# One product's form, a rider limit and a redrawn order of work in a gated mix of two attention blocks

## The chip, the cores and the metric

The kernel runs on one core of a Trainium2 chip. A core has five engines that run side by side, each through its own queue of instructions in order: PE (TensorE, matmuls, with a row PEld for the loading of weights), DVE (VectorE), ACT (ScalarE), POOL (GpSimd) and SP (SyncE, which here issues nearly all DMAs). The metric is the device time of one execution in microseconds. The time before is 739.46 us, the median of three runs (739.46, 739.46 and 740.83).

## What is computed

```python
def reference(A_x, A_wqkv, A_wo, B_x, B_wqkv, B_wo, gate_w):
    x = A_x                                     # [1, 2048, 512]
    g = sigmoid((x * gate_w).sum(-1, keepdims=True))
    a = A(x, A_wqkv, A_wo)     # full attention: 32 heads of 16, softmax over all 2048 keys
    b = B(x, B_wqkv, B_wo)     # 32 heads; each query sees 8 keys, at offsets 0, 2, ..., 14 behind it
    return g * a + (1 - g) * b
```

A and B each project x to q, k and v, attend, and multiply by their `wo`. B_x is not read. Nearly all the work is branch A's: 32 heads x 2048 x 2048 exponentials, and the two matmuls around them.

## The kernel before

**Branch A.** The 2048 queries are cut in 4 chunks of 512, the heads in 8 groups of 4. A *period* is one chunk with one group, 32 periods in all; within a period there are 16 key tiles of 128 by 4 heads, so 64 *units* of 128 keys x 512 queries of one head. For each unit PE writes the scores (tile `ring` or `m_ps`, in PSUM), an engine turns them into exponentials, and PE multiplies those by the values (tile `vp_row`) and adds them up in `acc`. Two engines make exponentials:

- ACT, which reads a whole *set* of ring banks with one instruction (`act_source`, tile `pT`). There are two sets, rA and rB, of three banks of 512 columns; a set holds three units of ACT, or two.
- DVE, in *quads*: the four heads of one key tile (`make_quad`, line 1673). Four conversions (`conv`, line 1707) turn scores into the bits of a power of two with one multiply and add; two further instructions (`term`, line 1723) add offsets to those bits, and PE adds the three terms with weighted copies of the values (`vd_row`). All these write tile `dt`.

The scores of a quad's head are filled either into the single bank `m_ps`, which all projections share too, or as a *rider* into the third bank of a ring set, whose other two banks then hold units of ACT (`rider`, line 1472; `take_ride`, line 1503). A set is filled again only when both ACT's exponential and the rider's conversion have read it.

**Branch B.** For each of 16 tiles of 128 queries (`b_tile`, line 945) PE projects q, k and v, the keys and values go to DRAM, and come back shifted (tiles `ksh`, `vsh`). POOL multiplies and adds up the scores (`prod`, `lg`), DVE takes maxima, ACT the exponentials, POOL weighs the values. In `sm_sum` (line 1093) DVE does three small things in a row: it sums the eight exponentials of each of 32 heads (`ssum`), takes the reciprocal (`rr`), and multiplies it in place by the column `ratio` of this tile (128 x 32 elements). POOL's `sm_norm` waits for that product.

**The order of work.** The kernel is written out by a planner (`Sched`) when the program is built. Every piece of work is an `Op` with an engine, a charged duration, what it depends on, buffers that it takes and gives back, and a due time; the planner simulates the five engines and issues the ops in the order in which it starts them. So each engine's queue has one fixed order, and a chain of no-sync dependencies keeps it. `sm_sum` is charged 900 ns as one op. DVE ops that are marked `lock` are kept clear of POOL's instructions; `sm_sum` is not one of them.

What the planner prefers is a `Policy` (line 125): how many quads may be open, how early or late things are pulled, how much PE is to stream before it adds matmuls on zeros (*zero passes*, `acc<-ones_t,zw`; the threshold is raised by `warm`). Time is cut in stretches of 8 us (`STRETCH`, line 68), and the table `CHOICES` gives a seed for each: a seed draws each setting with a chance of 0.3 from its other values; seed 0 takes the usual ones. `turn` (line 194) changes the policy at each stretch. Two settings matter here:

- `ride` (lines 136 and 156): a unit may ride if its conversion, at 683 ns, would end at most so many ns after the fill is visible (lines 1486 to 1489). Riders start after 17.5 us.
- `late` (lines 135 and 152): in `start_quad` (line 1641), `over` is the time that ACT still needs for the period (two periods, when looking one ahead), and `ends` is the time until DVE would have ended one more quad behind all that is due on it. Line 1661 skips the quad:

```python
            if over + S_.policy.late < ends:
                continue
```

All instructions carry line 511 in the profile, that of the helper which records them; they are told apart by their tiles.

Of the kernel before, what the change touches and what calls it, by code (L numbers as in the profile page):

```python
# [11 lines left out]
ALU = mybir.AluOpType  # L12
# [7 lines left out]
H = 32  # L20
# [16 lines left out]
def _mean_log_ratio():  # L37
    n = 4096
    acc = 0.0
    for k in range(n):  # L40
        y = 128.0 * k / n
        s = 0.0
        for o, w in zip(OFFS, WTS):
# [23 lines left out]

STRETCH = 8000.0
CHOICES = (
# [8 lines left out]
YIELD = 150.0  # L78
PARTS = ("k2", "q2", "v2", "bk2", "bv2", "bq2")
LRED = 4000.0  # L80
# [5 lines left out]
def _ap(base, dims):  # L86
    return bass.AP(tensor=base.tensor, offset=base.offset, ap=[list(d) for d in dims])


class Op:  # L90
# [4 lines left out]
    def __init__(self, eng, fn, dur=0.0, mms=None, deps=(), due=None, allow=1000.0, acq=(), rel=(), lat=0.0,  # L95
                 name="", not_before=0.0, after=None, begun=(), prompt=False,
                 lock=False):
        self.eng, self.fn, self.dur, self.mms = eng, fn, dur, mms
        self.deps = [d for d in deps if d is not None]
        self.due, self.allow, self.acq, self.rel, self.lat = due, allow, list(acq), list(rel), lat  # L100
        self.begun = [d for d in begun if d is not None]
        self.start = self.fin = self.vis = None
        self.prompt = prompt
        self.zeros = 0
        self.choose = None
        self.closing = False
        self.lock = lock
        self.gap = 30.0
        self.name, self.not_before, self.after = name, not_before, after
# [19 lines left out]
class Policy:  # L129
    __slots__ = ("full", "press", "quads", "backlog", "heed", "near", "shift", "conv", "ring", "rng", "wobble", "warm", "tight", "late", "whole", "split", "ride")  # L130

    def __init__(self, seed):
        self.full, self.press, self.quads, self.backlog, self.heed = 5, -2000.0, 3, 3000.0, True
        self.near, self.shift, self.conv, self.ring, self.wobble, self.warm = 60.0, 0.0, -5000.0, 480.0, 0.0, 0.0
        self.tight, self.late, self.whole, self.split = 600.0, 2000.0, False, False
        self.ride = 900.0
        self.rng = random.Random(seed)
        if seed:
            def pick(usual, *others):
                return self.rng.choice(others) if self.rng.random() < 0.3 else usual  # L140
            self.full = pick(5, 4)
            self.press = pick(-2000.0, -30000.0)
            self.quads = pick(3, 2, 4)
            self.backlog = pick(3000.0, 1500.0, 4500.0, 6000.0)
            self.heed = pick(True, False)
            self.near = pick(60.0, 20.0, 150.0)
            self.shift = pick(0.0, -4000.0, -2000.0, 2000.0, 4000.0)
            self.conv = pick(-5000.0, 0.0)
            self.ring = pick(480.0, 560.0, 650.0)
            self.wobble = pick(0.0, 500.0, 2000.0)  # L150
            self.tight = pick(600.0, 150.0, 1500.0)
            self.late = pick(2000.0, 0.0, 4000.0)
            self.whole = pick(False, True)
            self.split = pick(False, True)
            self.warm = pick(0.0, 0.04, 0.08, -0.03)
            self.ride = pick(900.0, 700.0, 1100.0)

    def move(self):
        return self.shift + self.wobble * (2.0 * self.rng.random() - 1.0)
# [288 lines left out]
def kernel(  # L448
# [66 lines left out]
    V = Chained(nc.vector, "dve")  # L515
# [72 lines left out]
    ratio = const.tile([128, NT], FP32, name="ratio")  # L588
# [356 lines left out]
    def b_tile(t, due):  # L945
# [147 lines left out]
        def sm_sum():  # L1093
            ssum = work.tile([128, H], FP32, name="ssum", tag="ssum", bufs=2)
            V.tensor_reduce(out=ssum[:], in_=st["lg"][:], axis=AX.X, op=ALU.add)
            rr = work.tile([128, H], FP32, name="rr", tag="rr", bufs=2)
            V.reciprocal(out=rr[:], in_=ssum[:])
            V.tensor_scalar(out=rr[:], in0=rr[:], scalar1=ratio[:, t:t + 1], scalar2=None, op0=ALU.mult)
            st["rr"] = rr

        def sm_norm():
# [2 lines left out]
        s_ = padd(sm_sub, 628.0, after_last=False, early=True, deps=[m_])  # L1104
        x_ = S_.add(Op("ACT", sm_exp, dur=391.0, allow=500.0, deps=[s_], name="smexp"))
        d_ = S_.add(Op("DVE", sm_sum, dur=900.0, allow=2500.0, deps=[x_] + g_done, name="smsum"))
        padd(sm_norm, 628.0, deps=[d_])

# [766 lines left out]
```

## Time and profile before

| | before |
|---|---|
| median of 3 runs | 739.46 us |
| the profiled execution | 737.08 us |
| its span, first to last instruction | 735.3 us |
| mean granted PE clock | 0.997 |
| busy share PE / DVE / ACT / POOL | 91% / 94% / 97% / 56% |
| exponentials on ACT | 648 instructions, 705.2 us |
| conversions on DVE, from ring and m_ps | 403 and 105 |

A line of a group reads: line, engine, operation, tile written <- tiles read, shapes and type, count | busy us in all, mean ns of one | idle time of the engine just before them and what ended it. Rows of a timeline give start and length in us, engine, operation, tiles, shapes and count, and in brackets how long the engine had been idle before, and who ended that. Rows of waits give who waited for whom: us in total, times, the longest.

### The profile page before, as it was taken

How to read it: one execution, taken by the hardware profiler on the slowest of the kernel's cores; microseconds unless marked ns; L12 is line 12 of the kernel's file. 1: busy time of each engine (PE TensorE's matmuls, PEld its weight loads, DVE VectorE, ACT ScalarE, POOL GpSimd, SP SyncE). 2: the span in 40 equal slices, each digit the busy share in tenths (PEclk: the TensorE clock that was granted, in tenths of full speed). 3: DMA queues.
4: the chain of work that ended last, by engine and by line, in shares of the span. 5: the costliest groups of instructions: out<-in, count | busy, mean ns of one | idle time of the engine just before them, and what ended most of it. 6: DMA issues, size and time to landing. Idle time of an engine off the chain costs nothing.

```text
span 735.3 us, 19566 instructions
## 1 busy us (share of the span) xinstructions
PE 672.6 (91%) x8164; PEld 247.3 (34%) x8164; DVE 690.4 (94%) x1234; ACT 713.8 (97%) x675; POOL 415.1 (56%) x418
## 2 busy tenths in 40 slices
PE   8999899989998989999989899899998999989997
PEld 4333232333323223333424233323333333323334
DVE  5999999999999999999799999999999999998994
ACT  4999999999999999999999999999999999999996
POOL 2036465565764656656656557566756676355560
PEclk9999999999999999999999999999999999999999
DMA  9242010030241303040112312120403030300300
GB/s 244 92 68 89 16 40 21 16 115 2 74 87 58 81 2 116 16 121 18 61 57 74 101 59 73 59 66 22 123 23 116 23 123 31 116 1 17 122 9 30
DMA packets 72312, 47.43 MB, mean 64 GB/s; under 512 B 33056, under 2 KB 69408, under 8 KB 72224
## 3 DMA queue, kind: packets, MB, share of 16 engines
q1 hardware_dynamic: 70496, 45.66, 21.0%
q8 instruction: 64, 1.05, 0.6%
q10 hardware_dynamic: 1728, 0.52, 0.3%
q14 instruction: 24, 0.20, 0.1%
HBM read 38.80 MB, written 6.32 MB: 61 GB/s over the span
## 4 chain that ended last, share of the span: by engine, by line
ACT 51%; DVE 25%; PE 11%; issue 10%; SPq 1%; DMA 0%; DVEq 0%; POOL 0%; ACTq 0%
ACT pT L511 51%; DVE dt L511 15%; PE ring L511 4%; PE m_ps L511 4%; PE acc L511 3%; DVE rr L511 2%; DVE kt_all L511 1%; DVE qt L511 1%; DVE lg L511 1%; SPq L511 1%; DVE kvs L511 1%; DVE accT L511 1%; DVE kmax_all L511 1%; DVE vp_row L511 1%; DMA xT<-in_A_x_dram 0%
## 5 line engine op out<-in xcount | busy, mean ns | idle before, releaser
L511 ACT ACTIVATE pT<-ring 128x1024 bf16<-128x1024 f32 (+1 forms) x648 | 705.2, 1285 | 6.5 <-PE ring L511 5.4
L511 PE MATMUL ring<-qt,kt_all 32*128 32x512 bf16 x1943 | 264.9, 383 | 42.0 <-ACT pT L511 30.1
L511 DVE TENSOR_SCALAR dt<-ring 128x512 uint16<-128x512 f32 x403 | 269.8, 677 | 15.1 <-PE ring L511 12.6
L511 POOL TENSOR_TENSOR prod<-ksh,qb 128x512 f32<-128x512 bf16 x128 | 145.5, 1156 | 114.9 <-DVE dt L511 94.2
L511 PEld LDWEIGHTS <-kt_all 32*128 32x128 bf16 (+1 forms) x2304 | 91.8, 91 | 276.2 <-issue 171.2
L511 DVE TENSOR_SCALAR dt<-dt 128x2048 uint16<-128x2048 uint16 x254 | 177.0, 710 | 1.2 <-PE acc L511 0.3
L511 POOL TENSOR_TENSOR vsh<-vsh,lg 128x512 bf16<-128x512 bf16 x128 | 137.4, 1098 | 69.6 <-DVE dt L511 54.3
L511 PE MATMUL acc<-pT,vp_row 128*32 128x512 bf16 x1540 | 156.5, 387 | 2.4 <-ACT pT L511 1.3
L511 POOL TENSOR_TENSOR prod<-prod 128x512 f32<-128x512 f32 x76 | 83.8, 1108 | 66.0 <-DVE dt L511 55.3
L511 PEld LDWEIGHTS <-vp_row 128*32 128x32 bf16 x2048 | 50.7, 94 | 98.6 <-issue 87.8
L511 PE MATMUL acc<-dt,vd_row 128*32 128x512 bf16 x1016 | 82.2, 380 | 0.0
L511 DVE TENSOR_SCALAR dt<-m_ps 128x512 uint16<-128x512 f32 x105 | 71.0, 676 | 0.5 <-PE ring L511 0.4
L511 PE MATMUL m_ps<-bw,xT 128*32 128x512 bf16 x768 | 55.4, 382 | 2.7 <-DVE dt L511 1.9
L511 PE MATMUL acc<-dt,vp_row 128*32 128x512 bf16 x508 | 50.4, 385 | 0.9 <-DVE accT L511 0.9
L511 PE MATMUL m_ps<-qt,kt_all 32*128 32x512 bf16 x105 | 39.9, 380 | 5.5 <-DVE dt L511 3.1
L511 PEld LDWEIGHTS <-xT 128*32 128x32 bf16 (+1 forms) x1088 | 32.9, 96 | 33.3 <-issue 26.6
L511 PE MATMUL m_ps<-ident,vsh 128*128 128x128 bf16 x512 | 37.9, 220 | 1.1 <-DVE dt L511 1.0
L511 DVE TENSOR_REDUCE lg<-prod 128x32 f32<-128x512 f32 x52 | 34.1, 671 | 0.0
L511 PEld LDWEIGHTS <-vsh 128*128 128x128 bf16 x512 | 29.1, 98 | 13.7 <-issue 12.6
L511 PEld LDWEIGHTS <-vd_row 128*32 128x32 bf16 x1016 | 26.1, 97 | 22.1 <-issue 7.7
L511 PE MATMUL acc<-ones_t,zw 128*32 128x512 bf16 x368 | 32.0, 385 | 0.1
L511 POOL TENSOR_TENSOR ott<-accT,rden 128x512 bf16<-128x512 f32 (+1 forms) x16 | 16.9, 1056 | 22.2 <-DVE dt L511 19.2
(94 smaller groups left out, 396.9 us busy)
## 6 DMA issues: line engine op xcount, KB each, us to landing
ksh<-kv_scr SPq DMA_DIRECT2D x16, 1024.0 KB, 5.4
vsh<-kv_scr SPq DMA_DIRECT2D x16, 1024.0 KB, 5.5
kv_scr<-kvs SPq DMA_DIRECT2D x16, 256.0 KB, 2.0
out_dram<-osb SPq DMA_DIRECT2D x14, 128.0 KB, 1.7
bw<-in_B_wqkv_dram SPq DMA_DIRECT2D x1, 1536.0 KB, 8.4
xn<-in_A_x_dram SPq DMA_DIRECT2D x2, 512.0 KB, 4.3
bwo<-in_B_wo_dram SPq DMA_DIRECT2D x1, 512.0 KB, 6.8
woarr<-in_A_wo_dram SPq DMA_DIRECT2D x8, 64.0 KB, 2.4
```

What stands on the lines that cost most here:

```text
L511: return chain_on(key, f(*a, **k))
```

## The change

Three places of the code change.

```diff
 CHOICES = (
-           0, 671811, 186164, 451001, 281332, 80945, 95777, 2725, 841250, 226619, 39723, 166693,
...
-           0, 741684, 0, 650854, 0, 988031, 0)
+           0, 0, 499928, 803669, 208658, 178077, 0, 998560, 158866, 788054, 313197, 966231,
...
+           13420, 0, 869455, 338121, 12097, 448362, 0)
@@ class Policy
-        self.ride = 900.0
+        self.ride = 1050.0
...
-            self.late = pick(2000.0, 0.0, 4000.0)
+            self.late = pick(2000.0, 0.0, 4000.0, -2000.0)
...
-            self.ride = pick(900.0, 700.0, 1100.0)
+            self.ride = pick(1050.0, 850.0, 1250.0)
@@ def sm_sum
-            V.tensor_scalar(out=rr[:], in0=rr[:], scalar1=ratio[:, t:t + 1], scalar2=None, op0=ALU.mult)
+            r1 = ratio[:, t:t + 1]
+            V.tensor_tensor(out=rr[:], in0=rr[:], in1=_ap(r1, [list(r1.ap[0]), [0, H]]), op=ALU.mult)
```

The product in `sm_sum` is written as a product of two tensors, of which the second is the column of the ratio read 32 times, in place of a product with a scalar per partition. The usual value of `ride` goes from 900 to 1050 ns, and its other values from 700 and 1100 to 850 and 1250; `late` may also be drawn as -2000. The table keeps its 91 entries of 8 us; 8 of them were 0, now 9 are. The new seeds draw `ride` 850 ten times, 1050 64 times and 1250 17 times (before: 700 ten, 900 59, 1100 22 times), `late` -2000 nine times, 0 15, 2000 57 and 4000 ten times (before: 0 twelve, 2000 69, 4000 ten times), and a raised `warm` 25 times (before 19). The charge for the clock that the change's name mentions stands in no line of the kernel.

12 rows, old and new, of the table CHOICES are left out of this document.

## The prediction

> **What bounds the kernel now.** I read the page first: the span, the busy shares, the chain that ended last.
>
> ```profile
> span 735.3 us, 19566 instructions
> PE 672.6 (91%) x8164; PEld 247.3 (34%) x8164; DVE 690.4 (94%) x1234; ACT 713.8 (97%) x675; POOL 415.1 (56%) x418
> ...
> ACT 51%; DVE 25%; PE 11%; issue 10%; SPq 1%; DMA 0%; DVEq 0%; POOL 0%; ACTq 0%
> ACT pT L511 51%; DVE dt L511 15%; PE ring L511 4%; PE m_ps L511 4%; PE acc L511 3%; DVE rr L511 2%; DVE kt_all L511 1%; DVE qt L511 1%; DVE lg L511 1%; SPq L511 1%; DVE kvs L511 1%; DVE accT L511 1%; DVE kmax_all L511 1%; DVE vp_row L511 1%; DMA xT<-in_A_x_dram 0%
> ```
>
> Two engines share the exponentials of branch A, and both are nearly full: ACT (tile pT) and DVE (tile dt). Next come two stretches, the middle of the run and 3.2 us out of it, then the mean clock. Columns: length, then for PE, PEld, DVE, ACT and POOL the busy time with its count, then granted clock, DMA share, GB/s.
>
> ```profile
> 25.00:700.00 675.00, 620.08 (x7501) 221.19 (x7500) 650.89 (x1156) 669.50 (x631) 396.35 (x387) 1.00 0.21 62
> ```
> ```profile
> 656.60:659.80 3.20, 3.20 (x30) 0.79 (x26) 2.18 (x5) 1.90 (x3) 1.09 (x1) 0.50 0.00 0
> ```
> ```profile
> core 0: 735.3 us, clock 0.997
> ```
>
> From 25 to 700 us ACT is idle for 675.00 - 669.50 = 5.5 us, DVE for 24.1 us. So the time is ACT's own work, and an order of work can gain only by giving ACT less of it or by removing stalls. One stall is plain: at half clock PE is busy throughout the 3.2 us and ACT idles 1.3 us of it, a quarter of its idle time in the 675. The mean clock of 0.997 leaves room for little beyond this one stretch.
>
> The groups kept apart by shape give the prices (count, then busy us and mean ns of one, then idle before):
>
> ```profile
> L511 ACT ACTIVATE pT<-ring 128x1024 bf16<-128x1024 f32 x404 | 404.4, 1122 | 4.1 <-PE ring L511 3.2 <-ACT pT L511 0.2
> L511 ACT ACTIVATE pT<-ring 128x1536 bf16<-128x1536 f32 x244 | 360.2, 1556 | 2.5 <-PE ring L511 2.2
> L511 DVE TENSOR_SCALAR dt<-ring 128x512 uint16<-128x512 f32 x403 | 269.8, 677 | 15.1 <-PE ring L511 12.6 <-PE m_ps L511 1.3
> ...
> L511 DVE TENSOR_SCALAR dt<-dt 128x2048 uint16<-128x2048 uint16 x254 | 177.0, 710 | 1.2 <-PE acc L511 0.3
> ...
> L511 DVE TENSOR_SCALAR dt<-m_ps 128x512 uint16<-128x512 f32 x105 | 71.0, 676 | 0.5 <-PE ring L511 0.4
> ...
> L511 PE MATMUL acc<-ones_t,zw 128*32 128x512 bf16 x368 | 32.0, 385 | 0.1
> ...
> L511 DVE TENSOR_SCALAR rr<-rr,ratio 128x32 f32<-128x32 f32 x16 | 11.0, 685 | 0.6
> ...
> L511 DVE TENSOR_REDUCE ssum<-lg 128x32 f32<-128x256 f32 x16 | 6.5, 405 | 0.0
> ...
> L511 DVE RECIPROCAL rr<-ssum 128x32 f32<-128x32 f32 x16 | 5.7, 353 | 0.6
> ```
>
> A unit is one head by 128 keys by 512 queries. ACT pays 1556/3 = 519 ns for a unit in a set of three, 1122/2 = 561 ns in a set of two. A set of two is one whose third bank a DVE unit rides in: 403 conversions read such a bank, 105 read the bank m_ps. **One rider** therefore costs ACT 1122 - 2 x 519 = 84 ns. **One quad** (four units on DVE) costs DVE 4 x 677 + 2 x 710 = 4.13 us; it takes 4 x 519 = 2.08 us off ACT, less 403/508 x 4 = 3.2 riders at 84 ns: 1.8 us. There are 254/2 = 127 quads.
>
> **Part one, the product.** Sixteen products of the normalizer with the ratio, 685 ns each. What they wait for shows in their spread (min/median/max) and in two places, one with POOL at work, one without:
>
> ```profile
> L511 DVE TENSOR_SCALAR rr<-rr,ratio x16: 242/590/1181, 96.1 to 704.5; 128x32 f32<-128x32 f32 x16
> ```
> ```profile
> 303.94 2.27 POOL L511 TENSOR_TENSOR prod<-ksh,qb 128x512 f32<-128x512 bf16 x2
> ```
> ```profile
> 305.07 1.18 DVE L511 TENSOR_SCALAR rr<-rr,ratio 128x32 f32<-128x32 f32 x1
> 306.17 0.68 DVE L511 TENSOR_SCALAR dt<-ring 128x512 uint16<-128x512 f32 x1
> ```
> ```profile
> 702.67 1.10 POOL L511 TENSOR_TENSOR vsh<-vsh,lg 128x512 bf16<-128x512 bf16 x1
> 706.06 0.63 POOL L511 TENSOR_TENSOR lg<-lg,rr 128x256 f32<-128x256 f32 x1 [2.29 <-DVE dt L511]
> ```
> ```profile
> 704.48 0.24 DVE L511 TENSOR_SCALAR rr<-rr,ratio 128x32 f32<-128x32 f32 x1
> ```
>
> The slow one ends at 306.25, where POOL's pair ends (306.21); the fast one falls where POOL is idle. So the product in its present form waits for the POOL instruction in progress, and a conversion stands behind it on DVE. The change writes it as a tensor by a tensor. Does that form wait too? The trace of before has four small ones, three at 160 ns, one at 914:
>
> ```profile
> L511 DVE TENSOR_TENSOR kadd<-kswap,rows x4: 160/160/914, 14.4 to 404.8; 128x2 f32<-128x2 f32 x4
> ```
> ```profile
> 360.94 1.15 POOL L511 TENSOR_TENSOR prod<-ksh,qb 128x512 f32<-128x512 bf16 x1
> ...
> 361.01 0.15 DVE L511 STREAM_SHUFFLE kswap<-kmax 128x1 f32<-128x1 f32 x1
> ...
> 361.20 0.91 DVE L511 TENSOR_TENSOR kadd<-kswap,rows 128x2 f32<-128x2 f32 x1
> ```
> ```profile
> L511 DVE TENSOR_TENSOR ott<-accT,rden x1: 424/424/424, 728.9 to 728.9; 128x256 bf16<-128x256 f32 x1
> ```
>
> The slow one ends at 362.11, and POOL's ended at 362.09; the shuffle ahead of it, with one input, did not wait. One sample, but to 20 ns the same end as in the form that is replaced. I conclude that both wait. The Trainium skill has this rule (SBUF — State Buffer, "Who interferes with whom"): a DVE instruction with two inputs in SBUF contends with a GpSimd instruction that reads SBUF, `tensor_tensor` included. By that rule the edit saves nothing wherever POOL is at work, and the 914 ns agree.
>
> Free of POOL, the new form costs 160 ns plus 30 elements at (424 - 160)/254 = 1.04 ns: 191 ns, 51 ns under 242. The median of 590 says that most of the sixteen waited; with three free ones: **-0.15 us**. The other bound: no wait at all, 16 x (685 - 191) = 7.9 us of DVE time. If it only makes room for quads, 7.9/(4.13 + 1.8) = 1.33 quads, 2.4 us; if every wait stood on the chain (where DVE rr has 2%), 7.9 us. The planner charges 900 ns for reduce, reciprocal and product together before and after, though they took 405 + 353 + 685 = 1443: this edit reorders nothing.
>
> **Part two, riders and late quads.** The limit up to which a conversion may end after its set's fill goes from 900 to 1050 ns by default; weighted by what the 91 seeds of the two tables draw, from 926 to 1065. An exponential of two units takes 1122, so the conversion still ends about when ACT leaves the set. What it risks and what it can win is in these waits (total us, times, longest):
>
> ```profile
> PE ring L511 <- ACT pT L511: 30.1, 98, 0.8
> ...
> PE ring L511 <- DVE dt L511: 8.1, 22, 0.8
> ...
> PE m_ps L511 <- DVE dt L511: 7.2, 15, 1.4
> ...
> ACT pT L511 <- PE ring L511: 5.4, 8, 1.3
> ```
>
> Fills already wait 22 times for a late conversion, yet ACT lost only 5.4 us to fills in all, 1.3 of them at half clock. So the added wait is covered by the set that ACT is reading meanwhile; without that cover, each of those 22 would pass its share of 8.1 us on. The price is the riders themselves, and ACT hides nothing: 0 to 105 more at 84 ns, 0 to +8.8 us. I take 20, a fifth of what is left, since the limit moves by 150 ns of a conversion's 677: **+1.7 us**. For it, the bank m_ps is freed 20 times of its 105, and DVE's 24.1 us of idle time can hold up to five quads (0 to -9 us); I take one: **-1.8 us**.
>
> The word "late" reads the wrong way round. The test skips a quad if ACT's remaining time plus this number is less than the time when DVE would end it, so the new value -2000 is the strictest, not the most lenient; nine seeds of 91 draw it, and the mean falls from 1956 to 1495. Fewer quads if anything: 0 to 3, 0 to +5.4 us. I take 0, since the other choices outweigh nine stretches.
>
> **Part three, the table.** It reorders everything after the first 8 us on every queue, SP's and POOL's too; the instructions themselves stay, except quads, riders and zero passes. What I can price is the clock. One half-clock stretch cost ACT 1.3 us. The three runs lie 1.37 us apart (739.46, 739.46, 740.83), and the profiled execution took 737.08 (735.3 and 1.8 around it), 2.4 under the median: 1.8 such stretches. I read the median as holding about 2.8 of them. The new table draws a raised fill threshold 25 times instead of 19, so a few more than the 92 zero passes (368/4); they fit into PE's 30.1 us of waiting for ACT. Bounds: all 2.8 go, -3.6 us; two more come, +2.6. I take two away: **-2.6 us**. (The Trainium skill, TensorE: Matmul & The Clock Gate, Terms, puts the penalty at throttled time x (1 - K/N), 1.7 us for 3.4 us at half rate; by that the term would be 3.4 us.)
>
> **Sum:** 739.46 - 0.15 + 1.7 - 1.8 - 2.6 = **736.6 us**.
>
> **Rivals.** (a) The product does not wait in its new place: between -2.4 and -7.9 I take -4 in place of -0.15, 732.7 us. For it: the kadd row is one sample, on two elements, and DVE rr does stand on the chain; against: its 914 ns. (b) Riders cost more than they bring, on ACT: half of the 105 move, 52 x 84 ns = +4.4, and no quad is added, while the clock keeps its stretches: 743.9 us. It decides from (1.8 + 2.6)/0.084 = 52 riders if the other terms hold, from any number if they do not. For it: ACT has only 5.5 us to absorb anything; against: riding frees the m bank. (c) The late value does the opposite of what it is called: three quads fewer, +5.4 - 2.6, 742.3 us; against: only nine stretches use it. (d) The redraw trades like for like and the clock stretches stay: 739.4 us.
>
> **How the numbers follow.** Forecast 0.43, (a) 0.08, (b) 0.20, (c) 0.13, (d) 0.16. The forecast's own range, by its bounds taken two at a time, is 733.5 to 738.5. The whole range reaches below (a), and above to (b): 730.5 to 744. About 0.2% (1.5 us) is what a measurement tells from no change. Faster: the forecast but for 0.03, (a), and a little of (d), 0.50; same 0.15; slower (b) and (c) with the rest, 0.35.
>
> **What would show it.** The product: tensor by tensor rows with a maximum near 1.1 us, ending with POOL's instructions; a flat 191 ns proves (a). Riders: the counts of 128x1024 and 128x1536 exponentials and of dt<-m_ps; 404 should grow by about 20, and more than 450 speaks for (b). Quads: dt<-dt, 254 now, 248 for (c). Clock: the granted clock at 1.00 in every stretch, and runs that agree with the profiled execution. The forecast is wrong if ACT's busy time moves by more than 4 us, or its idle time between 25 and 700 us leaves 3 to 8 us.

## The result and the profile after

| | before | after |
|---|---|---|
| median of 4 runs | 739.46 us (738.23 to 740.83) | 731.78 us (731.74 to 733.07) |
| profiled execution / its span | 737.08 / 735.3 us | 731.77 / 729.9 us |
| mean granted clock of the profiled execution | 0.997 | 0.999 |
| products with the ratio, 16 in all | 11.0 us | 8.1 us |

The ratio on record is 0.9915, the middle of its interval (0.989 to 0.994); the two medians themselves stand at 0.990. The medians lie 7.7 us apart: the time is inside the stated range, and the gain is more than twice the 2.9 us forecast. The page of the changed kernel:

```profile
span 729.9 us, 19605 instructions
## 1 busy us (share of the span) xinstructions
PE 669.5 (92%) x8187; PEld 248.7 (34%) x8187; DVE 683.3 (94%) x1234; ACT 712.3 (98%) x676; POOL 414.0 (57%) x418
...
ACT 60%; DVE 16%; issue 12%; PE 11%; DVEq 0%; ACTq 0%
```

Its span is 5.4 us shorter. ACT's busy time fell by 1.5 us (713.8 to 712.3), and its idle time by 3.9 us (21.5 to 17.6). The last line of the page is the chain that ended last: the work followed back from the last instruction, at each step to what released it. ACT stands for more of it, 60% for 51%, DVE for less, 16% for 25%. ACT's idle time fell between 25 and 700 us, where it is now 1.3 us instead of 5.5:

```profile
25.00:700.00 675.00, 621.88 (x7590) 225.59 (x7586) 647.79 (x1164) 673.73 (x640) 399.62 (x391) 1.00 0.21 62
```

The groups of the changed kernel that answer to the prices of before:

```profile
L511 ACT ACTIVATE pT<-ring 128x1024 bf16<-128x1024 f32 x407 | 404.6, 1139 | 0.9 <-PE ring L511 0.4
L511 ACT ACTIVATE pT<-ring 128x1536 bf16<-128x1536 f32 x242 | 354.8, 1562 | 1.7 <-PE ring L511 1.5
L511 DVE TENSOR_SCALAR dt<-ring 128x512 uint16<-128x512 f32 x407 | 273.1, 682 | 18.1 <-PE ring L511 16.4
...
L511 DVE TENSOR_SCALAR dt<-dt 128x2048 uint16<-128x2048 uint16 x254 | 173.7, 703 | 2.4 <-PE acc L511 1.9
...
L511 DVE TENSOR_SCALAR dt<-m_ps 128x512 uint16<-128x512 f32 x101 | 68.7, 680 | 1.0 <-PE m_ps L511 0.7
...
L511 PE MATMUL acc<-ones_t,zw 128*32 128x512 bf16 x388 | 34.6, 386 | 0.1
```

There are four more riders (407 for 403) and exactly as many quads (254/2 = 127), so the work is split between ACT and DVE as before. Five more zero passes run (388/4 = 97 for 92). The waits for late conversions are shorter: fills waited 13 times, 5.1 us, for 22 and 8.1; ACT waited 1.9 us for fills, for 5.4:

```profile
PE ring L511 <- DVE dt L511: 5.1, 13, 0.8
...
ACT pT L511 <- PE ring L511: 1.9, 4, 1.0
```

The products (min/median/max of one), and one that met a POOL instruction, from the timelines of DVE and of POOL:

```profile
L511 DVE TENSOR_TENSOR rr<-rr,ratio x16: 191/420/1049, 97.0 to 697.0; 128x32 f32<-128x32 f32 x16
```
```profile
451.71 0.93 DVE L511 TENSOR_TENSOR rr<-rr,ratio 128x32 f32<-128x32 f32 x1
```
```profile
451.50 1.10 POOL L511 TENSOR_TENSOR vsh<-vsh,lg 128x512 bf16<-128x512 bf16 x1
```

Free, it takes the 191 ns that were estimated. Behind POOL it waits: this one ends at 452.64, POOL's at 452.60. So the new form still waits for POOL, and yet a good deal of time was won. The experiments look for where.

### The profile page after: what moved, and what is told of

Its sections match the earlier page's. It is cut to its first block, busy times and chain, and to the rows that moved or that the text cites. A ratio compares the mean times of both kernels' runs of the same rounds, so it can differ in the third digit from the quotient of the medians.

```text
span 729.9 us, 19605 instructions
## 1 busy us (share of the span) xinstructions
PE 669.5 (92%) x8187; PEld 248.7 (34%) x8187; DVE 683.3 (94%) x1234; ACT 712.3 (98%) x676; POOL 414.0 (57%) x418
## 4 chain that ended last, share of the span: by engine, by line
ACT 60%; DVE 16%; issue 12%; PE 11%; DVEq 0%; ACTq 0%
ACT pT L511 60%; DVE dt L511 9%; PE ring L511 4%; PE acc L511 3%; PE m_ps L511 3%; DVE qt L511 1%; DVE lg L511 1%; DVE kt_all L511 1%; ACT lg L511 1%; DVE accT L511 1%; DVE rr L511 1%; DVE kmax_all L511 1%; PE warm L511 0%; DVE osb L511 0%; DVE vp_row L511 0%
## 5 line engine op out<-in xcount | busy, mean ns | idle before, releaser
L511 DVE TENSOR_SCALAR dt<-ring 128x512 uint16<-128x512 f32 x407 | 273.1, 682 | 18.1 <-PE ring L511 16.4
L511 PEld LDWEIGHTS <-kt_all 32*128 32x128 bf16 (+1 forms) x2307 | 94.1, 91 | 274.5 <-issue 172.3
L511 DVE TENSOR_SCALAR dt<-dt 128x2048 uint16<-128x2048 uint16 x254 | 173.7, 703 | 2.4 <-PE acc L511 1.9
L511 PE MATMUL acc<-pT,vp_row 128*32 128x512 bf16 x1540 | 150.5, 386 | 0.1
L511 DVE TENSOR_SCALAR dt<-m_ps 128x512 uint16<-128x512 f32 x101 | 68.7, 680 | 1.0 <-PE m_ps L511 0.7
L511 PE MATMUL m_ps<-qt,kt_all 32*128 32x512 bf16 x101 | 38.4, 380 | 3.9 <-DVE dt L511 1.7
L511 PE MATMUL acc<-ones_t,zw 128*32 128x512 bf16 x388 | 34.6, 386 | 0.1
```

The costliest lines, as they stand in the source:

```text
L511: return chain_on(key, f(*a, **k))
```

## The experiments

Each was timed against the kernel before on its chip, whose medians there were 738.63 (E1 to E4), 738.89 (E5 to E8) and 738.12 us (E9 and E10). The ratios are again the middles of their intervals.

| | order of work | product | median, us | ratio to before (95%) |
|---|---|---|---|---|
| E1 | old | DVE, two tensors | 736.38 | 0.9967 (0.9955 to 0.9979) |
| E2 | old | POOL | 730.68 | 0.9901 (0.9883 to 0.9919) |
| E3 | new | DVE, scalar | 731.80 | 0.9912 (0.9896 to 0.9928) |
| E4 | new | POOL | 730.38 | 0.9892 (0.9876 to 0.9908) |
| E5 | old | POOL, and 0.78 us of idle sums on DVE | 735.87 | 0.9959 (0.9945 to 0.9972) |
| E6 | new | POOL, and 0.78 us of idle sums on DVE | 734.82 | 0.9941 (0.9928 to 0.9953) |
| E7 | no table, limit 1050 | POOL | 761.56 | 1.0301 (1.0276 to 1.0326) |
| E8 | no table, limit 900 | POOL | 760.88 | 1.0304 (1.0281 to 1.0328) |
| E9 | old | the 8 long ones on POOL | 731.19 | 0.9910 (0.9892 to 0.9928) |
| E10 | old | the 8 short ones on POOL | 736.88 | 0.9984 (0.9968 to 1.0) |

### E1: the old order, only the product's form changed

```diff
-            V.tensor_scalar(out=rr[:], in0=rr[:], scalar1=ratio[:, t:t + 1], scalar2=None, op0=ALU.mult)
+            r1 = ratio[:, t:t + 1]
+            V.tensor_tensor(out=rr[:], in0=rr[:], in1=_ap(r1, [list(r1.ap[0]), [0, H]]), op=ALU.mult)
```

> The old order of work with the product alone rewritten as a product of two tensors. My theory: this form waits for POOL as the old one did, so the 16 products still reach about 1.1 us, their mean stays above 500 ns, and the time stays within 1 us of before (739.46). Rival (the product's form brought the gain): the products fall to a flat 191 ns and the time drops by 3 us or more.

736.38 us, 2.3 us under before: more than the theory allowed, less than the rival asked. Part of it goes with the granted clock: the one run of E1 at 1.000 took 735.00 us, the runs of before at 1.000 took 735.78 to 736.37, so at the same clock the form won about 1 us. The mean stayed at 10.0/16 = 628 ns and the maximum at 1175, so the waits are there:

```profile
L511 DVE TENSOR_TENSOR rr<-rr,ratio x16: 191/514/1175, 96.4 to 704.0; 128x32 f32<-128x32 f32 x16
```

One wait of before is gone, though, that of the eighth tile. In the kernel before (DVE, then POOL):

```profile
380.31 1.16 DVE L511 TENSOR_SCALAR rr<-rr,ratio 128x32 f32<-128x32 f32 x1
```
```profile
378.25 2.15 POOL L511 TENSOR_TENSOR vsh<-vsh,lg 128x512 bf16<-128x512 bf16 x2 [1.30 <-DVE dt L511]
380.36 1.08 POOL L511 TENSOR_TENSOR ott<-accT,rden 128x512 bf16<-128x512 f32 x1
```

And in E1:

```profile
381.80 0.19 DVE L511 TENSOR_TENSOR rr<-rr,ratio 128x32 f32<-128x32 f32 x1
```
```profile
380.80 1.10 POOL L511 TENSOR_TENSOR vsh<-vsh,lg 128x512 bf16<-128x512 bf16 x1
381.85 1.09 POOL L511 TENSOR_TENSOR ott<-accT,rden 128x512 bf16<-128x512 f32 x1
```

Both start about 50 ns before the next POOL instruction does, 90 to 100 ns before the one in progress ends (380.40 and 381.90). The old form waited until that next one had ended; the new form got through in 0.19 us, one sample. E10 shows the old form at the same place and offset once more, and it waited again:

```profile
381.37 1.17 DVE L511 TENSOR_SCALAR rr<-rr,ratio 128x32 f32<-128x32 f32 x1
```

Without a POOL instruction close behind, the old form at this offset does not wait: in E3 the product at 346.77 starts 90 ns before POOL's instruction ends, and takes 0.24 us.

### E2: the old order, the product moved to POOL

Here the product leaves DVE and stands in `sm_norm`, ahead of POOL's weighting; the planner's charges and its order stay.

```diff
-            V.tensor_scalar(out=rr[:], in0=rr[:], scalar1=ratio[:, t:t + 1], scalar2=None, op0=ALU.mult)
...
         def sm_norm():
+            r1 = ratio[:, t:t + 1]
+            G.tensor_tensor(out=st["rr"][:], in0=st["rr"][:], in1=_ap(r1, [list(r1.ap[0]), [0, H]]), op=ALU.mult)
             G.tensor_tensor(out=st["lg"][:], in0=st["lg"][:], in1=over_w(st["rr"]), op=ALU.mult)
```

> The old order with the product taken off DVE and done by POOL right ahead of its weighting of the eight exponentials. If the products' waits are what made conversions late and ACT stall in the old order, the ACT stalls at 308.6, 383.2 and 464.2 us, each some 3 us behind a product of 1.09 to 1.18 us, go, and the time falls by 2 to 5 us. If DVE had the time to spare, it stays within 1 us, and POOL's extra 16 instructions of about 0.25 us cost nothing.

730.68 us: 8 us, more than the 2 to 5 expected. This one line, in the old order, wins as much as the whole change. Some of it again goes with the clock, which was 0.999 or 1.000 in four of five runs; at 1.000 E2 took 730.44 to 730.93 us, about 5.5 less than before at 1.000. The products take 0.24 us on POOL, where they wait for nobody but the chain ahead of them. The chain that ended last shows what they had cost, DVE's share falling from 25% to 3%, and ACT's middle stretch idles 0.8 us instead of 5.5:

```profile
L511 POOL TENSOR_TENSOR rr<-rr,ratio x16: 233/239/245, 97.6 to 699.2; 128x32 f32<-128x32 f32 x16
```
```profile
ACT 77%; issue 13%; PE 5%; DVE 3%; SPq 1%; DMA 1%; DVEq 0%; ACTq 0%
```
```profile
25.00:700.00 675.00, 624.92 (x7575) 224.03 (x7575) 647.45 (x1152) 674.22 (x639) 403.85 (x407) 1.00 0.21 62
```

How one product cost ACT time can be followed in the kernel before, behind the slow product at 380.31. On DVE's timeline the conversions stand in a row behind it:

```profile
381.39 0.68 DVE L511 TENSOR_SCALAR dt<-m_ps 128x512 uint16<-128x512 f32 x1
381.99 0.68 DVE L511 TENSOR_SCALAR dt<-ring 128x512 uint16<-128x512 f32 x1
```

PE waited for them with its queue in order, a projection ahead of the ring set, and ACT waited for the set:

```profile
382.12 0.62 PE L511 MATMUL m_ps<-bw,xT 128*32 128x512 bf16 x8 [1.37 <-DVE dt L511]
382.67 0.39 PE L511 MATMUL ring<-qt,kt_all 32*128 32x512 bf16 x3
```
```profile
383.16 1.02 ACT L511 ACTIVATE pT<-ring 128x1024 bf16<-128x1024 f32 x1 [0.77 <-PE ring L511]
```

A product that takes 0.92 us longer than the free 0.24 comes out as 0.77 us of idle ACT about 2 us later. Not every long product does this. Of the seven over 0.7 us in that profile, four (at 225.0, 305.1, 380.3 and 461.2 us) have such a wait of ACT within 3 us of their end: 0.85, 0.23, 0.77 and 0.73 us, 2.6 us together. Behind the one at 653.0 comes the half-clock stretch, with ACT's 1.30 us; behind those at 179.4 and 508.2 ACT waits for no fill. So these waits are only a part of what E2 won. ACT's busy time also fell by 2.1 us (713.8 to 711.7) with the same instructions, and where that comes from was not traced.

### E3 and E4: the new order, with the old product and with the product on POOL

The edits are those of E1, backwards, and of E2, made in the changed kernel.

> The new order with the old form of the product. My theory: within 0.5 us of the changed kernel (731.78), since only the products that meet no POOL instruction are 51 ns shorter. Rival (the form matters): 3 us or more slower than the changed kernel.

> The new order with the product on POOL. The changed kernel has 8.1 us of products on DVE and few ACT stalls behind them; I expect 0 to 2 us under it, 730 to 731.8 us. If POOL's longer chain makes its tiles late, it is slower instead.

731.80 and 730.38 us, both as expected. In the new order the form changes nothing that can be measured (731.80 for 731.78, ratios 0.9912 and 0.9915). And with no product on DVE the two orders stand at 730.68 and 730.38: **apart from the products, the new order is no better than the old.** The products cost the old order 8.0 us and the new one 1.4. E4 is the shortest of all, but its interval overlaps those of E2 and E3, so the 1.4 us is itself hardly clear of the spread.

### E5 and E6: a fixed lateness in both orders

The product is on POOL, as in E2 and E4. In its place DVE sums twice into a spare tile, which no output reads:

```diff
             V.reciprocal(out=rr[:], in_=ssum[:])
+            idle = work.tile([128, H], FP32, name="idle", tag="idle", bufs=1)
+            for _ in range(2):
+                V.tensor_reduce(out=idle[:], in_=st["lg"][:], axis=AX.X, op=ALU.add)
```

> The old order with the product on POOL, and in its place on DVE two idle sums of 128x256 into a spare tile, one input each, which no POOL instruction can hold up: about 0.73 us more at each of the 16 places, as much as the old products took in the mean (0.685). If DVE's lateness there is the whole cost, this gives back what the move to POOL won: 736 to 740 us, with half-clock stretches back in most runs. If the cost lay in the waits on POOL themselves, it stays under 733.

> The new order with the same fixed lateness. Theory one, the new order stands lateness at these places better: it loses no more than 2.5 us against its form with the product on POOL (730.38). Theory two, the new order is no more tolerant and only met shorter waits (8.1 us of products instead of 11.0): it loses as much as the old order, 5 us or more.

735.87 and 734.82 us. In E5, as in E6, one idle sum took 391 ns in the mean:

```profile
L511 DVE TENSOR_REDUCE idle<-lg 128x32 f32<-128x256 f32 x32 | 12.5, 391 | 0.6
```

In the two runs each of the 32 took between 360 and 422 ns, most of them with POOL at work, so POOL did not hold them up as it did the products. 12.5 us of DVE time cost the old order 5.2 us (735.87 - 730.68) and the new one 4.4 (734.82 - 730.38); the two kernels of each pair ran on different chips, whose medians of before lie 0.3 us apart. E6 fell between the two theories' figures, nearer the second: the new order is hardly more tolerant. E5 came out just under its expected 736 to 740 us, and far over the 733 of the rival: lateness on DVE is enough to cost this much, without any wait on POOL. At a clock of 1.000 E5 (735.45 to 735.89) is nearly where before is (735.78 to 736.37). The expectation of half-clock stretches in E5 was a miss: four of its five runs were granted a clock of 1.000.

### E7 and E8: the rider limit by itself

`CHOICES` is cut to a single 0 in the kernel of E4; E8 also sets `ride` back to 900.

> All settings usual, no table drawn, rider limit 1050, product on POOL. If the limit itself brings something, this is 2 us or more faster than the same with 900; my theory is that the two differ by the order that happens to come out, in either direction, and that both lie over 10 us above the kernels with a table.

> All settings usual, no table drawn, rider limit 900, product on POOL. If the limit of 1050 brings something by itself, this is 2 us or more slower than the same with 1050; my theory is a difference in either direction, by the order that comes out, and over 10 us above the kernels with a table.

761.56 and 760.88 us, with intervals that overlap. Without a table the limit brings nothing that can be measured; what it does inside the new table was not separated. A drawn table is worth some 30 us to either, a part of which goes with the clock, which was 0.969 to 0.986 here.

### E9 and E10: the long products and the short ones

The edit of E2 under a condition on the tile: E9 moves the eight products that took 668 to 1181 ns in the profile of before, E10 the other eight.

```diff
+            if t in (2, 3, 5, 7, 8, 9, 10, 14):
+                r1 = ratio[:, t:t + 1]
+                G.tensor_tensor(out=st["rr"][:], in0=st["rr"][:], in1=_ap(r1, [list(r1.ap[0]), [0, H]]), op=ALU.mult)
```

> The old order; only the eight products that took 668 to 1181 ns in the profile of before (tiles 2, 3, 5, 7, 8, 9, 10, 14; 7.8 of the 11.0 us) go to POOL, the other eight stay on DVE in the old form. If a few long waits in bad places carry the cost, this wins most of what moving all sixteen won: 730.5 to 733 us, with the half-clock stretches gone from most runs. If the cost goes by the sum of DVE time alone, it wins 7.8/11.0 of it, with the rest spread: about 732.5 to 734.

> The complement: the eight short products (242 to 513 ns) go to POOL, the eight long ones stay on DVE. If the long waits carry the cost: 737 to 739 us, half-clock stretches still in most runs. If it goes by the sum: 735 to 736.5.

731.19 us is what was expected if the long waits carry the cost; 736.88 falls between the two figures named, close to that of the long waits (737 to 739). What stayed on DVE, in E9 and then in E10:

```profile
L511 DVE TENSOR_SCALAR rr<-rr,ratio x8: 241/420/511, 96.2 to 698.3; 128x32 f32<-128x32 f32 x8
```
```profile
L511 DVE TENSOR_SCALAR rr<-rr,ratio x8: 672/979/1165, 179.7 to 654.1; 128x32 f32<-128x32 f32 x8
```

Moving the eight long ones wins 6.9 us, the eight short ones 1.2, with an interval that reaches 1.0. In the changed kernel five products are over 0.7 us (at 97.0, 451.7, 574.2, 605.0 and 656.6 us), for seven before. After these ACT waits for a fill only twice, 0.41 us at 103.1 and 0.26 us at 659.4, against the 2.6 us of before. How many are long, and what stands behind them, is what the new order altered.

### The clock, over all runs of the kernel before

Each run comes with its mean granted clock. Thirty-six runs of the kernel before went with E1 to E10:

| granted clock | runs | time, us |
|---|---|---|
| 0.999 to 1.000 | 6 | 735.78 to 736.37 |
| 0.997 to 0.998 | 8 | 737.40 to 738.67 |
| 0.994 to 0.995 | 15 | 738.06 to 739.96 |
| 0.990 to 0.993 | 7 | 739.35 to 740.03 |

The stretch of half clock in the profile of before lies in this window, where the clock is the third figure from the end:

```profile
655.00:660.00 5.00, 4.27 (x41) 1.18 (x41) 3.98 (x8) 3.66 (x5) 1.58 (x2) 0.66 0.00 0
```

It lasted 5 x 0.34/0.5 = 3.4 us. One such stretch lowers the mean by 3.4 x 0.5/735 = 0.0023, so the rows step by about one stretch. Their medians are 735.95, 737.74, 738.63 and 739.59 us: each step goes with 0.9 to 1.8 us. The changed kernel's runs at 1.000 and 0.999 took 731.74 to 731.80, one at 0.996 took 733.07. So of the 7.7 us, **about 3.5 go with the clock** (739.46 - 735.98, where 735.98 is the median of the four runs at 1.000) and **about 4.2 are the work itself** (735.98 - 731.78). This is an estimate from a comparison of runs on several chips; no run changed the clock alone.

## Why the prediction was right or wrong

**The direction and the range held, the size did not.** 736.6 was forecast; 731.78 lies outside the forecast's own range of 733.5 to 738.5. One of the signs that it named for being wrong came true: ACT's idle time between 25 and 700 us is 1.3 us, under the 3 to 8; its busy time moved by 1.5 us, within the 4.

**The product: right, with an exception.** The two-tensor form waits for POOL (up to 1049 ns) and costs 191 ns when free, as was worked out from the `kadd` and `ott` rows. In the new order the form is worth nothing measurable (E3). In the old order it was worth 2.3 us (E1) and not 0.15, about 1 us of it at the same clock. The exception is a product that starts some 90 ns before a POOL instruction ends, with the next one close behind: there the new form got through.

**Riders, quads, late quads: the terms were too large, their sum was nearly right.** Taken were +1.7 for 20 riders and -1.8 for one quad; there were four riders and no quad, +0.3 us by the same prices. The near agreement of the sums, -0.1 and +0.3, is luck: two terms that did not occur cancelled. Rivals (b) and (c) fell: riders hardly grew, and the strict `late` cost no quad. Rival (d) was right that the redraw trades like for like, apart from the products (0.3 us between E2 and E4), but not that the clock stretches stay.

**The clock: the size was near, the reason is not borne out.** Two stretches fewer, -2.6 us, were taken from the spread of three runs; the 36 runs put what goes with the clock in the median at about 3.5 us, of which the changed kernel keeps next to nothing. That is the bound (-3.6) rather than the value. But the prediction linked it to the raised fill thresholds and a few more zero passes. E2, with the old table and its 368 matmuls on zeros, has the clock at 0.999 or 1.000 in four of five runs, so the extra passes were not needed: the stretches went when the products left DVE.

**The step that failed** is "What I can price is the clock", in part three. It priced the table by the clock alone and gave the order of work itself nothing. The product had been bounded at 2.4 to 7.9 us, but only for its form; that a new order would put the same waits elsewhere was not asked. E2 prices the products at 8.0 us in the old order, E4 at 1.4 in the new, the clock included: the 6.6 us between them are nearly all of the change, which comes to 6.8 us on the same chip (738.63 - 731.80). Rival (a) had the right place and nearly the right time (732.7), by the wrong way: the waits did not go, the long ones came more seldom and where less stood behind them. The rows for it had been quoted, the maximum of 1181 beside a median of 590, and 900 ns charged for three things that took 1443; read on from the 380 us product to the ACT wait 2 us later, they would have shown that a long product can pass most of its lateness on.

**What stays open.** Why the old order with its long products falls to half clock in most runs (in the profiles at 656 to 660 us before, at 197 to 201 in E1 and E10), while the same order with the products on POOL (E2) or an evenly spread lateness (E5) mostly does not, was not separated: long waits at certain places go with it, and E10, which keeps them, was at 0.991 to 0.998 in eight of twelve runs. Whether the higher clock charge helped the new table, or the table only fits by chance, can't be told from a kernel that doesn't contain the charge.

## What to carry to other kernels

When a small instruction of one engine shows a wide spread (242 to 1181 ns), follow its slowest places to the busiest engine, and price the wait there; some pass on most of their lateness (0.77 of 0.92 us here), others nothing. Before a schedule is redrawn around such a wait, try the instruction on the engine that it waits for: one line did in the old order what a new order did by other means. When a whole order of work is replaced, ask what it does to every wait that the planner does not charge.

## What the runs showed of the hardware

- A two-tensor product and one with a scalar per partition, both on 128x32 fp32 in SBUF, waited for the POOL product of two tensors in progress and ended about 40 ns after it (452.64 and 452.60 in the changed kernel). They differ at its end: 90 to 100 ns before it, the scalar form lost its turn to the next POOL instruction twice (1.16 and 1.17 us), the two-tensor form got through in 0.19 us (E1, once).
- Free of POOL the scalar form takes 241 ns (E9) and the two-tensor form 191 (the changed kernel); POOL does the same product in 0.24 us (E2).
- A sum of 128x256 with one input on DVE took 360 to 422 ns all 32 times, most of them with POOL at work (E5, E6).
